# Sliding-window attention with sinks and an RWKV channel mix on one Trainium2 core: the attention band packed into 64-key pieces, the value product in 64 x 64 tiles

## The chip, the core and the metric

The kernel runs on one core of a Trainium2 chip. The engines of that core work side by side and wait for each other by semaphores: PE (TensorE, matrix products, with its weight loads shown apart as PEld), DVE (VectorE), ACT (ScalarE), POOL (GpSimd) and SP (SyncE, which here only issues transfers). PE holds weights of up to 128 x 128 and streams the other operand past them; it can also be used as four quadrants of 64 x 64, each with weights and a stream of its own. The array's results go to PSUM, from which DVE and ACT read. Transfers between HBM and the on-chip SBUF run on 16 DMA engines.

The metric is the device time of the kernel in microseconds (us), the median of several runs, for the slowest core (here the only one).

## What is computed

```python
def _attn_ref(q, k, v, n_sink, window):          # B, H, S, D = 4, 8, 768, 64
    scale = 1.0 / np.sqrt(D)
    scores = scale * np.matmul(q, k.transpose(0, 1, 3, 2))
    pos = np.arange(S)
    is_sink = pos[None, :] < int(n_sink)         # n_sink = 4
    rel = pos[:, None] - pos[None, :]
    in_window = (rel >= 0) & (rel < int(window)) # window = 128
    scores = np.where(is_sink | in_window, scores, -1000000000.0)
...
    a = np.exp(scores)                           # softmax over the keys
...
    return np.matmul(a, v)

def _moe_ref(x, mu_k, mu_r, w_k, w_v, w_r):      # x: 4 x 768 x 512, heads side by side
    x_prev = ...                                 # x of the token before, zero at the start
    xk = mu_k * x + (1.0 - mu_k) * x_prev
    xr = mu_r * x + (1.0 - mu_r) * x_prev
    k = np.maximum(xk @ w_k, 0.0)                # 512 x 1024
    v = k * k @ w_v                              # 1024 x 512
    r = 1.0 / (1.0 + np.exp(-(xr @ w_r)))        # 512 x 512
    return r * v
```

The kernel's mask also keeps the four sink keys for queries that lie before them in the first rows, as the reference does. Inputs and output are float32, all matrix products run in bf16.

## The kernel before

The 4 sequences of 768 tokens are cut into 12 units of 256 queries: unit u is part T = u % 3 of sequence b = u // 3. The 8 heads go in 4 pairs (c or k in the code); a pair's two heads lie on the two halves of the 128 rows. A unit passes through four stages.

*Prepare.* Loads bring q, k and v of the unit as float32 (tiles qs, ks, vs, issued by SP at L462, L472, L479, L486). Casts to bf16 (qb, kb: L689, L693, L698; vb with an added column of ones: L770) run on ACT, POOL or DVE. Then q and k are transposed so that the head dimension lies on the rows (qt, kt): on PE (L733, L738), with an evacuation from PSUM, or, for k from unit 5 and q from unit 7 on, by a DMA transpose issued on SP (L715).

*Attend.* The scores are computed with keys on the rows and queries along the columns (tile sc in PSUM, two heads side by side, 512 columns each): L845, on 64 x 64 tiles (in unit 0 with whole 128-key weights). For one pair and each of the two heads, the 512 columns hold four blocks of 128 keys by 128 queries: the two diagonal blocks, the block one below, and the block that looks back into the unit before. Two pairs are done together. The exponential is taken by ACT (L917: 128 x 1024 elements, or 128 x 768 in a sequence's first unit, where nothing lies behind), and DVE multiplies the whole tile e by a mask of zeros and ones (L931). The value product L950 takes e as weights, 128 keys by 128 queries, and streams v with its column of ones, so that column 64 of the result is the softmax's denominator: 16 matmuls of 65 columns for two heads and 2 x 128 queries (12 in a first unit) add up in a PSUM bank. The four sink keys come in separately for T = 1 and 2 (scores L814 or L821, values L888 with whole-array weights or L903 in tiles), before the value product and into the same bank. DVE takes the reciprocal (L964) and multiplies (L967) into x.

*Mix.* x is transposed (on PE at L991, or by DMA at L1011) into xt; DVE forms td = x - x_prev (L1027) and the mixes xk and xr (L1040).

*Channel mix.* Key product L1117 (weights of 128 x 128 from w_k, 256 tokens streamed, 32 matmuls a unit), relu (L1127 on ACT or L1131 on DVE), square (L1139, DVE), gate product L1148, tanh (L1154, ACT; the sigmoid is got from it), value product L1166 (16 matmuls of 512 columns a unit), the final product with the gate (L1175, DVE; L1087 and L1097 are the last unit's own copies), and the store (L1182, L1102).

What sets the order: every operation gets a number as the program is built, and a table ORDER lists for each engine the numbers in the order in which it issues them; SP's list orders the loads, DMA transposes and stores. A table CHOICE says which engine takes an operation that has alternatives (a cast, a copy from PSUM, a relu, "PE/full" or "PE/tiles" for the sinks). The planner walks the lists with a table of costs, only to decide which buffer of a pool each tile gets: there are 2 score tiles sc, 5 tiles e, 4 PSUM banks for everything else, 3 staging tiles for each of q, k and v. An operation waits for its inputs and for its buffer. The weights come as float32 too: w_k in two halves of 1 MB (cast at L650 and L656, 128 x 1024 elements a piece), then w_r (1 MB) and w_v in two halves of 1 MB, all issued on SP at L505 through three staging tiles w.

```python
            P.op("ACT", act(width), expo, r, take=[("e", ek)], hold=[sck], reads=[sck],
                 writes=[ek])
...
            if u not in BIAS:
                P.op("DVE", dve(width, 0.52), masked, r, hold=[ek], port=True, writes=[ek],
                     reads=["mask" if T else "mask0"])
...
                            nc.tensor.matmul(out=o[:, g, a, :], lhsT=e[:, a, e0:e0 + 128],
                                             rhs=rhs, start=(T == 0 and i == 0),
                                             stop=(i == len(blocks) - 1), skip_group_check=True)
```

BIAS is empty in the kernel before, so that every unit has its mask. `take` claims a buffer, `hold` keeps one until the operation is done, `reads` and `writes` name what is waited for.

## Time and profile before

| | us | share of the span |
|---|---|---|
| timed runs: median of 3 (lowest to highest) | 166.36 (165.06 to 167.31) | |
| the profiled execution, span from first to last instruction | 163.8 | |
| PE busy | 154.4 | 94% |
| DVE busy | 148.4 | 91% |
| ACT busy | 121.4 | 74% |
| POOL busy | 32.7 | 20% |

The profiled execution shows only its span. What lies around the span (start and end of the kernel) is in the timed runs alone; against their median it is 2.5 us.

The page's second part cuts the span in 40 slices of 4.1 us; a digit is the busy share in tenths.

```profile
PE   7989779899999999999999999999999999999991
DVE  2589999999999999999999999998898989999931
ACT  3779899999999998999996689882499694152020
POOL 6643543222731022111103001032000100101001
```

PE has some free time in the first seven slices and next to none after; DVE is full from the fourth slice to the last but two; ACT has room in the second half, POOL nearly everywhere. A share of 91 or 94% alone doesn't say which engine sets the end: for that, the stretches and the chain of waits are needed.

How to read the rows that follow. In a row of the group view stand line, engine, operation, output<-inputs, shape and count, then after the bar the busy time of all in us and the mean duration of one in ns, and after the second bar the engine's idle time just ahead of them, with what ended it. A row of the time line has start, duration, engine, line and operation, both times in us. A row of the chain of waits has start, duration, engine, what is written and the line. A row of transfers has the output<-input, the queue that issued it, the count, the size of each and the median time from issue to landing. "SPq" is SP's queue as an issuer of transfers.

### The profile page before, as it was taken

Reading aid. Unit: us, or ns where it says so; the run is one execution under the profiler, and the core shown is the slowest. Engines: PE = TensorE matmul, PEld = TensorE weight load, DVE = VectorE, ACT = ScalarE, POOL = GpSimd, SP = SyncE. Lnnn points to the kernel's source line nnn. Section 1 sums busy time; section 2 is a strip of 40 time slices with the busy share of each in tenths; the row PEclk is TensorE's granted clock in tenths of the full one; section 3 lists DMA queues with packets and bytes.
Section 4 is the critical chain, followed back from the end, with each engine's and each line's share of the span. In section 5 each row is a group of like instructions: output and inputs, shape, how many; then the busy total and the mean of one; then the engine's idle time right before and its main releaser. Section 6 shows DMA issues by size and latency. Waiting matters only on the chain.

```text
span 163.8 us, 4680 instructions
## 1 busy us (share of the span) xinstructions
PE 154.4 (94%) x1845; PEld 100.8 (62%) x1845; DVE 148.4 (91%) x383; ACT 121.4 (74%) x198; POOL 32.7 (20%) x61
## 2 busy tenths in 40 slices
PE   7989779899999999999999999999999999999991
...
DVE  2589999999999999999999999998898989999931
ACT  3779899999999998999996689882499694152020
POOL 6643543222731022111103001032000100101001
...
GB/s 138 250 334 275 400 346 205 362 397 338 200 289 238 265 233 225 196 179 189 276 233 174 254 196 218 242 188 119 239 162 201 268 79 98 57 203 64 0 144 112
DMA packets 78821, 35.16 MB, mean 215 GB/s; under 512 B 68744, under 2 KB 71056, under 8 KB 78800
## 3 DMA queue, kind: packets, MB, share of 16 engines
...
q0 software_dynamic: 400, 1.31, 2.3%
q8 instruction: 14, 0.23, 0.6%
q14 instruction: 7, 0.06, 0.1%
q10 hardware_dynamic: 16, 0.00, 0.0%
HBM read 24.12 MB, written 6.29 MB: 186 GB/s over the span
## 4 chain that ended last, share of the span: by engine, by line
PE 69%; DVE 11%; DMA 10%; SPq 5%; issue 2%; ACT 1%; POOL 0%; DVEq 0%; POOLq 0%
PE bank L1117 22%; PE bank L1166 19%; PE bank L1148 9%; PE bank L950 6%; DMA ks<-in_k_dram 5%; PE sc L845 4%; DMA kt<-kb 4%; DVE e L931 3%; SPq L462 3%; PE bank L1232 3%; DVE xk L1040 2%; DVE x L967 2%; PE bank L903 1%; SPq L479 1%; PE bank L991 1%
## 5 line engine op out<-in xcount | busy, mean ns | idle before, releaser
L1117 PE MATMUL bank<-xk,wk_sb 128*128 128x256 bf16 x384 | 47.3, 273 | 0.7 <-ACT rl L1127 0.5
L917 ACT ACTIVATE e<-sc 128x1024 bf16<-128x1024 f32 (+1 forms) x48 | 44.4, 966 | 3.4 <-PE sc L845 3.3
L1166 PE MATMUL bank<-wv_h,kk 128*128 128x512 bf16 x184 | 44.9, 379 | 0.0
L1117 PEld LDWEIGHTS <-wk_sb 128*128 128x128 bf16 x384 | 36.2, 98 | 7.0 <-issue 0.9
L931 DVE TENSOR_TENSOR e<-e,mask 128x1024 bf16<-128x1024 bf16 (+1 forms) x48 | 31.7, 676 | 0.0
L1127 ACT ACTIVATE rl<-bank 128x512 bf16<-128x512 f32 x43 | 25.1, 606 | 8.1 <-PE bank L1117 7.9
L1154 ACT ACTIVATE th<-bank 128x512 f32<-128x512 f32 x24 | 14.3, 608 | 18.2 <-PE bank L1148 11.4
L1166 PEld LDWEIGHTS <-kk 128*128 128x128 bf16 x184 | 17.0, 98 | 16.4
L1148 PE MATMUL bank<-wr_sb,xr 128*128 128x512 bf16 x96 | 23.8, 379 | 0.0
L1040 DVE SCALAR_TENSOR_TENSOR xk<-td,mu_all,xt 128x256 bf16<-128x256 bf16 x48 | 23.2, 511 | 0.0
L1040 DVE SCALAR_TENSOR_TENSOR xr<-td,mu_all,xt 128x256 bf16<-128x256 bf16 x48 | 22.4, 477 | 0.0
L967 DVE TENSOR_TENSOR x<-bank,rec 128x256 bf16<-128x256 f32 x48 | 19.5, 418 | 0.5
L1139 DVE TENSOR_TENSOR kk<-rl 128x512 bf16<-128x512 bf16 x48 | 19.3, 416 | 0.3 <-ACT rl L1127 0.2
L1175 DVE SCALAR_TENSOR_TENSOR ob<-th,bank 128x512 f32<-128x512 f32 x23 | 15.6, 682 | 2.4 <-PE bank L1166 1.1
L950 PE MATMUL bank<-vb,e 128*128 128x65 bf16 x352 | 16.5, 194 | 0.3
L950 PEld LDWEIGHTS <-e 128*128 128x128 bf16 x352 | 13.8, 97 | 3.5 <-DVE e L931 0.7
L1148 PEld LDWEIGHTS <-xr 128*128 128x128 bf16 x96 | 9.0, 98 | 9.6
L845 PE MATMUL sc<-qt,kt 64*64 64x128 bf16 (+3 forms) x496 | 12.6, 226 | 0.4 <-DMA kt<-kb 0.3
L1182 POOL DMA_DIRECT2D out_dram<-ob x5 | 2.8, 570 | 47.0 <-DVE ob L1175 47.0
L845 PEld LDWEIGHTS <-kt 64*64 64x64 bf16 (+1 forms) x496 | 9.0, 106 | 4.1 <-issue 1.4
L1027 DVE TENSOR_TENSOR td<-xt 128x512 bf16<-128x512 bf16 x24 | 10.1, 433 | 0.1
L770 ACT CAST vb<-vs 128x512 bf16<-128x512 f32 x14 | 8.8, 636 | 0.2 <-DMA vs<-in_v_dram 0.2
...
## 6 DMA issues: line engine op xcount, KB each, us to landing
vs<-in_v_dram SPq DMA_DIRECT2D x24, 256.0 KB, 5.5
out_dram<-ob SPq DMA_DIRECT2D x18, 256.0 KB, 3.4
ks<-in_k_dram SPq DMA_DIRECT2D x16, 256.0 KB, 4.6
qs<-in_q_dram SPq DMA_DIRECT2D x12, 256.0 KB, 4.7
...
w<-in_moe_w_k_dram SPq DMA_DIRECT2D x2, 1024.0 KB, 8.8
w<-in_moe_w_v_dram SPq DMA_DIRECT2D x2, 1024.0 KB, 11.3
```

What stands on the lines that cost most here:

```text
L845: nc.tensor.matmul(out=sc[keys, a, o0 + f0 - q0:o0 + f1 - q0], lhsT=lhs[rows, keys], rhs=qs[rows, f0:f1], start=u not in BIAS, stop=True, ...
L917: nc.scalar.activation(out=buf[ek][:, :, lo:], in_=buf[sck][:, :, lo:], func=AF.Exp, scale=scale)
L931: nc.vector.tensor_tensor(out=at, in0=at, in1=m, op=ALU.mult)
L950: nc.tensor.matmul(out=o[:, g, a, :], lhsT=e[:, a, e0:e0 + 128], rhs=rhs, start=(T == 0 and i == 0), stop=(i == len(blocks) - 1), skip_gro ...
L967: P.op("DVE", dve(256), lambda ok=ok, rk=rk, c=c: nc.vector.tensor_tensor(out=buf["x", u][:, :, 128 * c:128 * c + 128].rearrange("p g (a d ...
L1040: nc.vector.scalar_tensor_tensor(out=buf[key][:, c, :], in0=buf[tk][:, i, :], scalar=mu[w][:, c:c + 1], in1=xt[:, c, t0 - 1:t0 + 255], op0 ...
L1117: nc.tensor.matmul(out=ps[:, i, :], lhsT=wk_sb[:, c, 128 * f:128 * f + 128], rhs=xk[:, c, :], start=(c == 0), stop=(c == NC - 1), skip_gro ...
L1127: nc.scalar.activation(out=buf[rk], in_=buf[psk].rearrange("p (i t) -> p i t", i=2), func=AF.Relu)
L1139: P.op("DVE", dve(512, 0.52), lambda f2=f2, rk=rk: nc.vector.tensor_tensor(out=buf["kk", u][:, 2 * f2:2 * f2 + 2, :], in0=buf[rk], in1=buf ...
L1148: nc.tensor.matmul(out=buf[psk], lhsT=buf["xr", u][:, c, 128 * g:128 * g + 128], rhs=wr_sb[:, c, :], start=(c == 0), stop=(c == NC - 1))
L1166: nc.tensor.matmul(out=buf[psk], rhs=wv_h[:, f, :], lhsT=buf["kk", u][:, f, 128 * g:128 * g + 128], start=(f == 0), stop=(f == NF - 1))
L1175: P.op("DVE", dve(512), lambda psk=psk, tk=tk, bk=bk: nc.vector.scalar_tensor_tensor(out=buf[bk], in0=buf[tk], scalar=1.0, in1=buf[psk], o ...
```

## The change

**Packing.** The band of 128 keys back is cut into pieces of 64 keys by 64 queries. For each head, and for each half h of the 128 rows (even 64-key blocks on rows 0 to 63, odd ones on rows 64 to 127), six such pieces lie side by side in 384 columns, at places given by a table `slot`. Pieces that lie outside the band have no place any more. In each half the pieces at places 0, 3 and 2, 5 are the triangles (the edge of the window, seen from either side); places 1 and 4 need no mask. So sc is used for 2 x 384 columns instead of 2 x 512, e has that size, the exponential always takes 128 x 768 elements (L1005), and the mask multiplies only 2 x 2 x 2 x 64 = 512 elements a row (L1015).

**Triangles by matmul.** In units 0, 1 and 2 (BIAS) there is no mask. There, 4 more matmuls a pair (48 in all, on 64 x 64 tiles, 256 columns each, L898) add -30000 to the triangles in PSUM, ahead of the exponential. The tables for this are made on POOL at the start, with the new masks; the identity now comes before them.

**Values in tiles.** The value product (L923) takes e as weights of 64 keys by 64 queries and streams 65 columns of v: 24 matmuls a pair (20 in a first unit) instead of 8 (6), on the four quadrants. Two pairs are done in two halves: in the first, key rows 0 to 63 work on the first pair and rows 64 to 127 on the second; in the second half, the other way about, into the same PSUM bank rows. Between the halves stands `tick`, a memset of one element on POOL (L1026), made to wait for the first half's last matmul; the second half's first matmul is made to wait for it.

**Sinks** all go in tiles ("PE/tiles"). WHOLE is gone: unit 0 too is done in tiles.

**Order.** ORDER, CHOICE and the places where PE's instruction fetches are expected (FETCH) are new throughout. Five stores that POOL issued go to SP ("SP" in CHOICE). PE has 5376 instructions (weight loads among them) where it had 3679.

```diff
+BIAS = (0, 1, 2)
...
-BIAS = ()
...
-WHOLE = (0,)
...
-    pool("e", 5, [128, 2, 512], BF16)
+    pool("e", 5, [128, 2, 384], BF16)
...
+    def behind(one, other):
+        tc.add_manual_dep(one.ins, other.ins.name, mybir.DependencyInfo(
+            mybir.DependencyClass.Sync, mybir.DependencyReason.DATA))
...
+    scratch = tile1([1, 1], FP32, "scratch")
...
+        slot = [{(0, 0): 0, (0, 1): 1, (0, 2): 2, (2, 2): 3, (2, 3): 4},
+                {(1, 1): 0, (1, 2): 1, (1, 3): 2, (3, 3): 3}]
+        if T > 0:
+            slot[0][-2, 0] = 5
+            slot[1][-1, 0], slot[1][-1, 1] = 4, 5
+        else:
+            slot[0][0, 3] = 5
...
+            spans = [[(0, 0, 3), (2, 2, 4)], [(1, 1, 4), (3, 3, 4)]]
...
+                        nc.tensor.matmul(
+                            out=sc[64 * h:64 * h + 64, a, c0:c0 + 64 * (i1 - i0)],
+                            lhsT=keys[rows, k, kb // 2 % 2, 64 * h:64 * h + 64],
+                            rhs=qs[rows, 64 * i0:64 * i1], start=u not in BIAS or n == 0,
+                            stop=u not in BIAS, skip_group_check=u in BIAS)
+            if u not in BIAS:
+                return
+            for a in range(2):
+                rows = slice(64 * a, 64 * a + 64)
+                for h in range(2):
+                    nc.tensor.matmul(
+                        out=sc[64 * h:64 * h + 64, a, 0:384].rearrange(
+                            "p (t s w) -> p t s w", t=2, s=3)[:, :, 0:3:2, :],
+                        lhsT=ident[rows, rows],
+                        rhs=(bias[rows].unsqueeze(1).to_broadcast([64, 2, 2, 64]) if T else
+                             bias0[rows, h]), start=False, stop=True, skip_group_check=True)
...
+        def values(cs, second):
+            todo = [[], [], [], []]
+            for h in range(2):
+                c = cs[(h + second) % 2]
+                for (kb, i), n in sorted(slot[h].items(), key=lambda x: (x[0][1], x[0][0])):
+                    for a in range(2):
+                        todo[2 * h + i % 2].append((kb, i, n, a, c))
...
+                        new = nc.tensor.matmul(
+                            out=buf["o", u, c][64 * m:64 * m + 64, o0:o0 + D + 1],
+                            lhsT=buf["e", u, c][rows, a, 64 * at:64 * at + 64],
+                            rhs=buf["vb", u if kb >= 0 else u - 1][rows, kb // 2 % 2, 2 * c + a, :],
+                            start=T == 0 and not second and (c, m) not in begun,
+                            stop=bool(second), skip_group_check=True)
+                        if second and not begun:
+                            behind(new, halves[u, cs[0]])
...
-            P.op("ACT", act(width), expo, r, take=[("e", ek)], hold=[sck], reads=[sck],
+            P.op("ACT", act(768), expo, r, take=[("e", ek)], hold=[sck], reads=[sck],
...
+                at = buf[ek].rearrange("p a (t s w) -> p (a t) s w", t=2, s=3)[:, :, 0:3:2, :]
+                m = (mask.unsqueeze(1).to_broadcast([128, 4, 2, 64]) if T else
+                     mask0.rearrange("p a t s w -> p (a t) s w"))
...
-                P.op("DVE", dve(width, 0.52), masked, r, hold=[ek], port=True, writes=[ek],
+                P.op("DVE", dve(512, 0.52), masked, r, hold=[ek], port=True, writes=[ek],
...
+                        def tick(at=(u, cs[0])):
+                            new = nc.gpsimd.memset(scratch, 0.0)
+                            behind(new, halves[at])
+                            halves[at] = new
```

The first place that the new order moves is SP's queue of loads at the start, before the channel mix. The first listing shows the rows of the kernel before around the loads of w_k (w_76 and w_77 are the staging tiles; ks, qs, vs are those of k, q and v; the names in brackets are the semaphores that the issue waits for).

```order
L479 DMA ks_69<-in_k_dram 128x2x512 [waits DMAHW5_49]
L505 DMA w_76<-in_moe_w_k_dram 128x4x512 [waits DMAHW6_49]
L505 DMA w_77<-in_moe_w_k_dram 128x4x512 [waits DMAHW7_49]
L479 DMA qs_70<-in_q_dram 128x2x512 [waits DMAHW0_49,DVE_49,Activation_49]
L462 DMA vs_75<-in_v_dram 128x8x64 [waits DMAHW1_49]
L462 DMA vs_75<-in_v_dram 128x8x64 [waits DMAHW2_49]
L479 DMA ks_67<-in_k_dram 128x2x512 [waits DMAHW3_49,Pool_49]
L505 DMA w_78<-in_moe_w_r_dram 128x4x512 [waits DMAHW4_49]
```

The second listing shows the same queue of the changed kernel, from the third unit's loads to w_r.

```order
L507 DMA ks_67<-in_k_dram 128x2x512 [waits DMAHW6_49,DVE_49]
L490 DMA vs_75<-in_v_dram 128x8x64 [waits DMAHW7_49]
L507 DMA qs_71<-in_q_dram 128x2x512 [waits DMAHW0_49,Activation_49,Pool_49]
L490 DMA vs_75<-in_v_dram 128x8x64 [waits DMAHW1_49]
L507 DMA qs_70<-in_q_dram 128x2x512 [waits DMAHW2_49,Pool_49]
L533 DMA w_76<-in_moe_w_k_dram 128x4x512 [waits DMAHW3_49]
L507 DMA qs_72<-in_q_dram 128x2x512 [waits DMAHW4_49,Activation_49,Pool_49]
L507 DMA ks_68<-in_k_dram 128x2x512 [waits DMAHW5_49]
L533 DMA w_77<-in_moe_w_k_dram 128x4x512 [waits DMAHW6_49]
```

w_k's first half has moved behind the loads of ks_67, both of vs_75, qs_71 and qs_70; its second half also behind qs_72 and ks_68. Ahead of the first half stand 6.0 MB where 4.0 stood, and the two halves no longer stand together.

The second place is POOL in the middle of the program, around the copies of the third sequence's sink keys (ksink from kt). Before, POOL has only casts (kb, qb, vb) and copies there.

```order
L693 CAST kb_79<-ks_67 128x4x128 [waits DMAHW6_49,DVE_49,PE_49]
L770 CAST vb_136<-vs_75 128x8x64 [waits DMAHW1_49]
L787 COPY ksink_151<-kt_87 64x4x4 [waits DMAHW4_49]
L787 COPY ksink_151<-kt_87 64x4x4 [waits Pool_49]
L693 CAST kb_80<-ks_68 128x4x128 [waits PE_49,DMAHW5_49,Activation_49,Pool_49]
L693 CAST kb_81<-ks_69 128x4x128 [waits DMAHW3_49,DMAHW0_49]
L693 CAST qb_84<-qs_72 128x4x128 [waits DMAHW5_49,PE_49,Activation_49]
```

In the changed kernel the ticks stand between them in the same queue.

```order
L729 CAST qb_82<-qs_70 128x4x128 [waits DMAHW2_49,DMAHW5_49,DVE_49,Activation_49]
L1026 MEMSET scratch 1x1 [waits PE_49,Pool_49]
L823 COPY ksink_154<-kt_87 64x4x4 [waits DMAHW4_49]
L823 COPY ksink_154<-kt_87 64x4x4 [waits Pool_49]
L729 CAST qb_84<-qs_72 128x4x128 [waits DMAHW0_49,Pool_49]
L1026 MEMSET scratch 1x1 [waits PE_49]
L1026 MEMSET scratch 1x1 [waits PE_49,Pool_49] x2
L729 CAST qb_83<-qs_71 128x4x128 [waits DMAHW1_49,Activation_49]
L1026 MEMSET scratch 1x1 [waits PE_49,Pool_49] x2
```

Each memset waits for PE, stands behind whatever cast POOL issues before it, and is waited for by the first weight load of a second half on PE; six of the 24 come before PE's first matmul of the channel mix, 18 after.

251 lines of the change are left out of this document (134 added, 117 removed), and 141 rows, old and new, of the table ORDER.

## The prediction

> **What bounds the kernel now.** I read the page's first lines, then cut the span at two events: the first matmul of the channel mix (L1117, its key product) and the first value product (L1166).
>
> ```profile
> span 163.8 us, 4680 instructions
> L1117 PE MATMUL bank<-xk,wk_sb x384: 269/273/283, 24.3 to 151.4; 128*128 128x256 bf16 x192
> L1166 PE MATMUL bank<-wv_h,kk x184: 377/379/390, 41.1 to 158.6; 128*128 128x512 bf16 x184
> 0.00:24.30 24.30, 19.77 (x242) 11.32 (x243) 19.07 (x55) 18.68 (x29) 12.47 (x32) 1.00 0.97 291
> 24.30:41.10 16.80, 15.94 (x215) 11.77 (x211) 16.73 (x44) 16.27 (x27) 4.51 (x5) 1.00 1.03 323
> 41.10:160.30 119.20, 118.72 (x1396) 77.75 (x1394) 112.03 (x285) 86.47 (x144) 15.38 (x26) 1.00 0.87 186
> 21.52 1.31 DVE e L931 x2
> ```
>
> The two rows with "x384:" and "x184:" give when those lines first ran. The three rows of stretches give start and end, length, the busy time of PE, its weight loads, DVE, ACT and POOL, the granted clock (1.00 is full), the DMA share and GB/s; the last row is one of the chain of waits. They say: up to 24.3 us PE waits (its busy time there holds warm-up matmuls) and the chain of waits runs through DVE, the masks of L931 among it; from 24.3 to 41.1 PE, DVE and ACT are all full; from 41.1 to 160.3 PE is busy 118.72 of 119.20 us. So after the first channel-mix matmul the end is PE's own work, and a microsecond saved on DVE or ACT there is worth nothing by itself. The sum is: when PE can begin the channel mix, plus what PE has to do from there.
>
> **Prices on PE.** Consecutive starts in the time line, and merged rows of the chain, give what one group occupies.
>
> ```profile
> 57.92 0.31 PE L903 MATMUL bank<-vsink,es 64*64 64x130 bf16 x8
> 58.06 0.51 PE L845 MATMUL sc<-qt,kt 64*64 64x192 bf16 x24
> 58.50 0.66 PE L950 MATMUL bank<-vb,e 128*128 128x65 bf16 x16
> 59.00 0.39 PE L733 MATMUL bank<-ident,qb 128*128 128x128 bf16 x4
> 59.22 0.38 PE L1166 MATMUL bank<-wv_h,kk 128*128 128x512 bf16 x1
> 49.16 1.31 PE bank L1117 x12
> 56.27 1.73 PE bank L1148 x8
> 70.63 0.23 PE bank L888 x4
> 58.17 0.40 PE L845 MATMUL sc<-qt,kt 64*64 64x128 bf16 x16
> ```
>
> Eight tiled sink matmuls take 0.14, 24 tiled scores 0.44, 16 value matmuls of 128 x 128 0.50 (0.031 each), four transposes 0.22, a channel-mix matmul 0.109 (L1117) or 0.216, four full sinks 0.23. Switching between 64 x 64 tiles and the whole array costs about 0.09: the last scores end at 58.57 (58.17 + 0.40), and the first whole-array matmul starts 0.07 before that, whereas within one mode a matmul starts 0.16 before its predecessor ends (379 ns of duration against 216 of spacing). So the scores themselves are 0.35. Each of the four quadrants streams 768 columns in them: 0.456 ns a column.
>
> **The values.** A half now is 24 matmuls of 65 columns on four quadrants (20 in a sequence's first unit); the busiest quadrant has 8 (6), so 520 (390) columns: 0.237 (0.178), against 0.50 (0.38) for the 16 (12) before, which two halves replace. Values alone are a gain of 0.03 per two pairs. What is added with them is a round trip in the middle: the second half starts only after a POOL memset that waits for the first half.
>
> ```profile
> 58.72 0.76 POOL L693 CAST kb<-ks 128x512 bf16<-128x512 f32 x1 [5.32 <-PE sc L845]
> 0.34 0.10 POOL L1271 MEMSET const-float32-1.0<- 128x1 f32 x1
> 7.47 0.61 POOL L698 CAST kb<-ks 128x512 bf16<-128x512 f32 x1 [1.52 <-DMA ks<-in_k_dram]
> 8.13 0.40 PE L738 MATMUL bank<-ident,kb 128*128 128x128 bf16 x4 [0.38 <-POOL kb L698]
> L950 PE MATMUL bank<-vb,e 128*128 128x65 bf16 x352 | 16.5, 194 | 0.3
> ```
>
> POOL starts 0.15 after the scores' end (58.57), a memset takes 0.10, PE starts 0.05 after a POOL instruction's end (7.47 + 0.61), and a 65-column matmul ends 0.19 after its start: 0.49 for the trip. Of the 18 trips after the first channel-mix matmul, 16 have the next two pairs' scores between the halves (0.35 and 0.02 of spacing), one the sink scores and one two products. So 17 expose about 0.12, **2.1** in all (between 0, if PE pulls its weights early, and 0.3 each). Behind a second half wait the rest of PE's queue, and DVE's reciprocals and x (L964, L967).
>
> **PE's work after the first channel-mix matmul**, counted in PE's order: the three products of the channel mix are the same. Values go from 296 to 36 halves (24 of the larger kind): 9.2 becomes 7.8, so -1.4. Score groups go from 19 to 17, -0.7. Transposes (L733, L991) go from 92 to 60, -1.8. Three full sink groups go and one tiled comes, -0.5. Switches go from 44 to 49, +0.5. Together **-3.9**: this work now stands ahead of that matmul, or is gone. The triangles by matmul (48, in units 0 to 2) are all ahead of it. So are 15 of 20 added switches.
>
> **When that matmul can start.** Its weights now stand behind 6.0 MB of loads, not 4.0.
>
> ```profile
> 13.68 1.16 SPq L505 DMA_DIRECT2D w<-in_moe_w_k_dram  x2
> w<-in_moe_w_k_dram SPq DMA_DIRECT2D x1, 1024.0 KB, 7.8
> 15.62 4.56 SPq L462 DMA_DIRECT2D vs<-in_v_dram  x2
> vs<-in_v_dram SPq DMA_DIRECT2D x2, 256.0 KB, 10.9
> 25.49 0.72 SPq L505 DMA_DIRECT2D w<-in_moe_w_r_dram  x1
> w<-in_moe_w_r_dram SPq DMA_DIRECT2D x1, 1024.0 KB, 7.0
> 22.45 1.11 ACT L650 ACTIVATE wk_sb<-w 128x1024 bf16<-128x1024 f32 x1
> ```
>
> Each pair of rows is an issue and its time to landing. The first half of wk landed at 21.5 as the fifth megabyte; the seventh was complete with v of unit 2, the second transfer of its row, at about 27.2; w_r, with which 8.5 MB were complete, at 32.5. The queue was full throughout (DMA share 0.97 and 1.03), so I take landing by bytes: wk's first half, now megabyte seven, at 27.2, its cast 1.1 later, the matmul at 28.4 and not 24.3: **+4.1** (+2 if the queue fills sooner, +6 if PE still has attention to do). Its second half completes megabyte nine, half a megabyte after the last mark: 1.6 later at 323 GB/s, so 34.1, castable by 35.2; PE wants it after 32 key matmuls, two transpose groups, a score group, more transposes and sink scores, 5.3 later (33.7): **+1.5**. Against that, PE's work between the two events before came to 15.0 by the prices above in 16.8 us; those 1.8 of waits were for weights and for masks and go, **-1.8**. Of PE's later waits I take off **0.5** for faster ACT and DVE:
>
> ```profile
> L1117 PE MATMUL bank<-xk,wk_sb 128*128 128x256 bf16 x384 | 47.3, 273 | 0.7 <-ACT rl L1127 0.5 <-DVE xk L1040 0.2
> L917 ACT ACTIVATE e<-sc 128x1024 bf16<-128x1024 f32 x32 | 31.8, 1037 | 2.2 <-PE sc L845 2.1
> L917 ACT ACTIVATE e<-sc 128x768 bf16<-128x768 f32 x16 | 12.6, 825 | 1.2 <-PE sc L845 1.2
> L931 DVE TENSOR_TENSOR e<-e,mask 128x1024 bf16<-128x1024 bf16 x32 | 22.9, 727 | 0.0
> L931 DVE TENSOR_TENSOR e<-e,mask 128x768 bf16<-128x768 bf16 x16 | 8.9, 573 | 0.0
> L1139 DVE TENSOR_TENSOR kk<-rl 128x512 bf16<-128x512 bf16 x48 | 19.3, 416 | 0.3 <-ACT rl L1127 0.2
> ```
>
> The exponentials fall to 48 of 825 ns (-6.8). The masks fall from 31.8 to 36 of 512 elements, 0.42 each by the equally long kk row (-16.7); casts, copies and relus that now run on DVE give back about 8. Both gains lie beside PE's work after 28.4, where that work covers them; ahead of it they let PE finish three units' attention instead of two and a half, which the -3.9 holds already.
>
> Sum: 163.8 + 4.1 + 1.5 - 1.8 - 0.5 - 3.9 + 2.1 = 165.3, and 0.3 for the one short-covered trip (sink scores, 0.22): 165.6. The three timed runs have a median of 166.36 and run from 165.06 to 167.31, 2.5 above the span at the median. Adding 1.8 to the median gives 168.2: no change that a measurement can tell, since about 2% (163.0 to 169.7) is what it can.
>
> **The rivals.**
>
> *Faster: the front wins.* The early loads here are mostly 2-KB pieces, so the queue may fill sooner: the matmul at 26.4 (-2.0), no wait for the second half (-1.5), the trips hidden (-2.4): 162.3. For it speaks that the first stretch's DMA share was 0.97 with 291 GB/s against 323 in the second; against it, that all three must come together.
>
> *Slower: the memset is stuck in POOL's line.* Nine of the 18 memsets stand directly behind a cast or copy that waits for a load or another engine.
>
> ```profile
> POOL vb L770 <- DMA vs<-in_v_dram: 19.9, 5, 12.6
> L693 POOL CAST kb<-ks 128x512 bf16<-128x512 f32 x6 | 4.0, 664 | 19.7 <-DMA ks<-in_k_dram 10.4 <-PE sc L845 7.4 <-ACT xt L1000 1.9
> ```
>
> The first row gives POOL's waits for v (sum, count, longest): up to 12.6 us at a time, and that cost nothing; now PE waits with it. It decides once a load lands after the first half of the values: nine casts of 0.6 on average are +5.0: 173.2.
>
> *Slower: the tiles' weights.* Only the sinks reload all four quadrants in every wave, at 0.07 a wave; were a value wave to take that, halves cost 0.56 and 0.42, +10: 178. The scores, with 24 loads in 0.35, speak against it.
>
> The Trainium skill (TensorEngine Tiling (Array Packing), Gotcha 2: Feature Incompatibilities) says that column tiling excludes the fast weight load, and its page TensorE: Matmul & The Clock Gate (LDWEIGHTS) puts a load at one column per cycle of 1.2 GHz, 53 ns for 64 columns. By that estimate a wave would last 53 ns and not 30, and the kernel 174.7; the trace's loads of 14 ns apiece in the scores do not bear it out, but there only some quadrants reload at once.
>
> *Slower: the last keys.* The last unit's first scores have 33.0 us of PE work behind them by these prices, 29.7 before.
>
> ```profile
> 125.30 1.23 SPq L715 DMA_TRANSPOSE kt<-kb  x1
> kt<-kb SPq DMA_TRANSPOSE x7, 3.9
> 130.36 0.46 PE sc L845 x16
> ```
>
> Their transpose was issued at 125.3, to land by about 129; a PE that ends at 162.1 wants them at 128.9. Five stores more on that queue could make it 3 later: 171.
>
> *The relief does nothing.* If DVE and ACT relief is worth more than I took, 166: still no change.
>
> **Chances.** Forecast 0.45; the front 0.18; POOL's line 0.19; tile weights 0.07; last keys 0.06; more relief 0.05. So faster 0.18, within 2% 0.45 + 0.05 = 0.50, slower 0.32. The range runs from the front's 162.0 to POOL's 173.5; outside lie the tile weights and parts of the two rivals at its ends, under 0.2. Over the forecast's own terms it is 165 to 170.
>
> **What would show it.** The first channel-mix matmul at 28.4 rather than 24.3; between halves some 0.12 of PE idle, released by POOL; values near 0.24 a half; PE busy to the end with DVE near 85% of the span. I am wrong if PE has gaps of half a microsecond behind POOL, if wk lands near 21, or if value waves come slower than 30 ns.

## The result, and the profile after

The changed kernel takes 177.38 us (median of 4 runs, 175.44 to 178.61), the kernel before 166.62 us on the same chip: slower by a ratio of 1.062 (95% interval 1.053 to 1.071). The forecast was 168.2, with a range up to 173.5. (Ratios here leave out executions that were disturbed, so one can lie a little below the ratio of its medians.)

First the answers that correspond to those shown of before: the page's head of the changed kernel, the row of the channel mix's key product (L1187, which was L1117), and the stretches. The stretches are cut at the first transposes, the first transpose of x, the first key product, the first value product (L1236, which was L1166) and PE's end; the columns are those of the prediction.

```profile
span 175.8 us, 6387 instructions
...
PE 160.1 (91%) x2673; PEld 107.1 (61%) x2695; DVE 141.3 (80%) x382; ACT 109.5 (62%) x185; POOL 32.8 (19%) x98
```

```profile
L1187 PE MATMUL bank<-xk,wk_sb x384: 272/273/283, 37.8 to 165.1; 128*128 128x256 bf16 x192
```

```profile
0.00:7.55 7.55, 4.63 (x7) 2.00 (x7) 3.31 (x17) 2.10 (x3) 5.89 (x26) 1.00 0.70 203
7.55:20.89 13.34, 11.84 (x220) 8.25 (x219) 6.33 (x15) 8.71 (x14) 6.64 (x22) 1.00 1.14 308
20.89:37.80 16.91, 12.70 (x406) 9.87 (x405) 12.87 (x36) 12.38 (x21) 4.49 (x12) 0.90 0.82 293
37.80:54.85 17.05, 16.59 (x222) 12.90 (x222) 16.29 (x41) 15.30 (x26) 5.41 (x7) 1.00 0.95 259
54.85:172.30 117.45, 114.38 (x1828) 74.12 (x1846) 102.08 (x275) 70.96 (x122) 10.34 (x32) 1.00 0.87 170
```

The same cut of the kernel before, where its first stretch of 24.3 us is split in three:

```profile
0.00:4.70 4.70, 3.57 (x4) 1.27 (x5) 1.70 (x8) 1.50 (x3) 3.38 (x14) 1.00 0.53 154
4.70:12.63 7.93, 6.86 (x63) 3.81 (x62) 5.71 (x21) 6.35 (x10) 3.67 (x12) 1.00 1.04 298
12.63:24.30 11.67, 9.34 (x179) 6.25 (x177) 11.67 (x28) 10.83 (x18) 5.42 (x6) 1.00 1.11 342
```

The first key product came at 37.8 us and not at 24.3: 13.5 later, of which 2.85 stand ahead of the first transposes, 5.4 ahead of the first transpose of x and 5.2 behind it. From there to PE's end it is 134.5 us, 136.0 before, so that part gained 1.5. The span grew by 12.0, which is 13.5 less 1.5. The whole loss lies ahead of the channel mix, and there PE was idle: busy 12.70 of 16.91 in the third stretch, while DVE, full before (11.67 of 11.67), also waited.

What PE waited for: first its time line around the two largest gaps (start, length, operation; in brackets the idle time in front and its cause), then SP's with the loads of weights, the time from issue to landing of w_k's first half, and the casts of w_k (lengths in ns, first and last start).

```profile
24.72 0.36 PE L888 MATMUL sc<-qt,kt 64*64 64x192 bf16 x12
26.59 0.30 PE L898 MATMUL sc<-bias,ident 64*64 64x256 bf16 x4 [1.51 <-issue]
...
30.80 0.28 PE L898 MATMUL sc<-bias,ident 64*64 64x256 bf16 x4
32.79 0.31 PE L991 MATMUL bank<-vsink,es 64*64 64x130 bf16 x8 [1.70 <-ACT qb L725]
```

```profile
20.20 0.60 SPq L533 DMA_DIRECT2D w<-in_moe_w_k_dram  x1
...
23.48 0.78 SPq L533 DMA_DIRECT2D w<-in_moe_w_r_dram  x1
37.23 0.37 SPq L533 DMA_DIRECT2D w<-in_moe_w_v_dram  x1
```

```profile
w<-in_moe_w_k_dram SPq DMA_DIRECT2D x1, 1024.0 KB, 7.6
```

```profile
L686 ACT ACTIVATE wk_sb<-w x2: 1060/1060/1060, 36.1 to 42.4; 128x1024 bf16<-128x1024 f32 x2
```

The first half of w_k was issued at 20.20 and landed 7.6 later, at 27.8, yet its cast began only at 36.1: the weights lay there for 8 us, and the channel mix waited for something else. In the first gap nothing that the profile shows was waited for ("issue", between instructions of one score group). The second gap is put down to a cast that has nothing to do with sinks. Both fall on a pattern that appears when PE's instructions (weight loads and matmuls) are counted in order and the packets of the instruction queue (q8, 16 KB each) are set beside them. The table is worked out from the traces: the number of the instruction, when the one ahead of it started, the gap up to it, and the first fetch after it; the fetch that ends a gap stands a row higher.

```
kernel    instr.  reached   gap    next fetch
before       449    22.90   0.00   25.70-26.86
before       705    33.25   0.11   36.08-37.14
after        449    20.26   0.41   24.26-25.31
after        705    24.89   1.70   30.45-31.57
after        961    30.81   1.97   33.94-34.88
```

The gaps fall on instructions 449, 705 and 961, 256 apart, which is 16 KB a block. PE resumed 1.3 and 1.2 us after the end of a fetch (25.31 to 26.59, and 31.57 to 32.78). That this is no accident shows in all the traces of this case together: they hold 28 gaps of over 1 us at these numbers and at 1217, in 13 runs, and every one ends 1.2 to 1.6 us after the end of a fetch, whatever the other engines have just finished. Blocks came about 6 us apart (24.26, 30.45), and each fetch began 3.6 to 3.9 us after PE had entered a block (20.67, 26.59), while loads kept the DMA engines full. The kernel before reaches its first key product as instruction 488, the changed one as 1259: small tiles mean many instructions, and half a unit more of attention stands ahead.

One thing more stands in the third stretch: the granted clock is 0.90 there, which was 1.00 throughout before. In steps of 2 us:

```profile
32.00:34.00 2.00, 1.21 (x58) 0.89 (x58) 0.27 (x1) 1.44 (x3) 0.09 (x1) 1.00 0.94 342
34.00:36.00 2.00, 1.74 (x40) 1.38 (x38) 1.90 (x7) 1.41 (x3) 0.00 (x0) 0.57 0.15 59
36.00:38.00 2.00, 2.00 (x74) 1.92 (x66) 2.00 (x6) 1.21 (x3) 1.36 (x4) 0.57 0.04 8
38.00:40.00 2.00, 2.00 (x23) 1.81 (x22) 1.94 (x7) 2.00 (x4) 1.95 (x3) 1.00 0.59 208
```

From 34 to 38 us PE runs at 0.57 of its clock (0.5 in the middle), right behind its gaps. The same rows show the loads run dry (8 GB/s): SP stood at the load of w_v from 24.3 to 37.2 us, since its staging tile held the w_k that was not yet cast.

### The profile page after: what moved, and what is told of

Its sections match the earlier page's. It is cut to its first block, busy times and chain, and to the rows that moved or that the text cites. A ratio compares the mean times of both kernels' runs of the same rounds, so it can differ in the third digit from the quotient of the medians.

```text
span 175.8 us, 6387 instructions
## 1 busy us (share of the span) xinstructions
PE 160.1 (91%) x2673; PEld 107.1 (61%) x2695; DVE 141.3 (80%) x382; ACT 109.5 (62%) x185; POOL 32.8 (19%) x98
## 4 chain that ended last, share of the span: by engine, by line
PE 70%; DMA 9%; DVE 7%; issue 4%; POOL 3%; ACT 2%; SPq 2%; DVEq 0%; POOLq 0%; ACTq 0%
PE bank L1187 19%; PE bank L1236 18%; PE bank L1218 10%; PE bank L923 8%; PE sc L888 4%; DMA kt<-kb 3%; PE bank L769 3%; DMA ks<-in_k_dram 3%; DMA qt<-qb 3%; DVE xr L1110 2%; PE bank L1061 2%; PE bank L991 2%; POOL hmask L604 1%; SPq L1081 1%; PE sc L898 1%
## 5 line engine op out<-in xcount | busy, mean ns | idle before, releaser
L1187 PE MATMUL bank<-xk,wk_sb 128*128 128x256 bf16 x384 | 48.7, 273 | 0.0
L1236 PE MATMUL bank<-wv_h,kk 128*128 128x512 bf16 x172 | 43.9, 379 | 1.7 <-DVE kk L1209 0.7
L1005 ACT ACTIVATE e<-sc 128x768 bf16<-128x768 f32 x48 | 37.7, 814 | 8.0 <-PE sc L898 4.4
L1187 PEld LDWEIGHTS <-wk_sb 128*128 128x128 bf16 x384 | 36.6, 98 | 9.6
L1197 ACT ACTIVATE rl<-bank 128x512 bf16<-128x512 f32 x37 | 21.5, 599 | 24.5 <-PE bank L1187 21.3
L1236 PEld LDWEIGHTS <-kk 128*128 128x128 bf16 x184 | 17.2, 98 | 18.2 <-DVE kk L1209 0.7
L1110 DVE SCALAR_TENSOR_TENSOR xr<-td,mu_all,xt 128x256 bf16<-128x256 bf16 x48 | 23.8, 506 | 0.0
L923 PE MATMUL bank<-vb,e 64*64 64x65 bf16 x1088 | 20.7, 197 | 1.2 <-DVE kt L787 0.7
L923 PEld LDWEIGHTS <-e 64*64 64x64 bf16 x1088 | 16.3, 109 | 5.7 <-issue 2.3
L1026 POOL MEMSET scratch<- 1x1 f32 x24 | 2.5, 105 | 89.7 <-PE bank L923 86.0
L946 DVE RECIPROCAL rec<-bank 128x4 f32<-128x4 f32 x48 | 7.1, 171 | 11.0 <-PE bank L923 10.7
L888 PE MATMUL sc<-qt,kt 64*64 64x64 bf16 (+2 forms) x544 | 15.4, 226 | 0.5 <-DMA kt<-kb 0.4
L1015 DVE TENSOR_TENSOR e<-e,mask 128x512 bf16<-128x512 bf16 x36 | 14.5, 418 | 0.0
L888 PEld LDWEIGHTS <-kt 64*64 64x64 bf16 x544 | 12.1, 110 | 2.2 <-DVE kb L734 0.8
```

What stands on the lines that cost most here:

```text
L888: nc.tensor.matmul(out=sc[64 * h:64 * h + 64, a, c0:c0 + 64 * (i1 - i0)], lhsT=keys[rows, k, kb // 2 % 2, 64 * h:64 * h + 64], rhs=qs[rows ...
L923: new = nc.tensor.matmul(out=buf["o", u, c][64 * m:64 * m + 64, o0:o0 + D + 1], lhsT=buf["e", u, c][rows, a, 64 * at:64 * at + 64], rhs=bu ...
L1005: nc.scalar.activation(out=buf[ek], in_=buf[sck][:, :, 0:384], func=AF.Exp, scale=scale)
L1015: nc.vector.tensor_tensor(out=at, in0=at, in1=m, op=ALU.mult)
L1110: nc.vector.scalar_tensor_tensor(out=buf[key][:, c, :], in0=buf[tk][:, i, :], scalar=mu[w][:, c:c + 1], in1=xt[:, c, t0 - 1:t0 + 255], op0 ...
L1187: nc.tensor.matmul(out=ps[:, i, :], lhsT=wk_sb[:, c, 128 * f:128 * f + 128], rhs=xk[:, c, :], start=(c == 0), stop=(c == NC - 1), skip_gro ...
```

## The experiments

Each kernel is the changed kernel with the edit shown, and lines of code may be shifted by it (L1187 is L1194 or L1200 below). "First key product" is the start of its first matmul in the one profiled execution. Times are medians, with the ratio to the kernel before in the same session and its 95% interval. How far a single start can be trusted shows in the changed kernel itself: a second profile of it, further down, has 37.04 where the first has 37.80.

**GpSimd's constants.** Before the change POOL built ident first; after it, the triangles and masks stand ahead of it (rows of the changed kernel, then of before):

```profile
1.28 0.92 POOL L604 TENSOR_SCALAR_AFFINE_SELECT mask<-ones 64x64 bf16<-64x64 bf16 x4 [0.77 <-DVE ones L588]
2.25 0.92 POOL L604 TENSOR_SCALAR_AFFINE_SELECT bias<-warm 64x64 bf16<-64x64 bf16 x4
3.25 2.11 POOL L604 TENSOR_SCALAR_AFFINE_SELECT hmask<-hmask 128x260 bf16<-128x260 bf16 x4
...
6.86 0.28 POOL L604 TENSOR_SCALAR_AFFINE_SELECT ident<-ones 128x128 bf16<-128x128 bf16 x1
```

```profile
2.31 0.28 POOL L573 TENSOR_SCALAR_AFFINE_SELECT ident<-ones 128x128 bf16<-128x128 bf16 x1
```

Identity first, in the order of POOL's operations (72 is ident, 75, 76 and 78 are masks):

```diff
-        75, 73, 78, 76, 72, 79, 74, 132, 101, 77, ...
+        72, 75, 73, 78, 76, 79, 74, 132, 101, 77, ...
```

> Changed kernel with one move on POOL: the identity is made first, ahead of the masks, the triangles and hmask. Theory A (POOL's constants hold up the front): the identity is ready near 2.1 us instead of 7.5, the first transposes start near 5.1 (when k's first cast ends) instead of 7.55; but the triangles of unit 0 (bias0) are still ready only near 9.3, and the first scores, at 10.27 before, wait for them, so the first channel-mix matmul comes only 0 to 1 us earlier than 37.8, and the time falls by 0 to 1 from 177.4. Theory B (the forecast: w_k's landing and cast set that matmul) and theory C (the attention of three units that PE's order puts ahead of it sets it): no change, first channel-mix matmul 37.5 to 38.

Identity first and the band's masks behind the first units' casts:

```diff
-        75, 73, 78, 76, 72, 79, 74, 132, 101, 77, ..., 141,
+        72, 73, 74, 78, 79, 132, 101, 77, ..., 141, 75, 76,
```

> Changed kernel with POOL's order changed at the start: identity, triangles of units 0 to 2, hmask, then the casts of q; the masks, which no unit before the fourth reads, go behind the first cast of v of unit 1. Theory A: bias0 is ready near 4.6, first transposes near 5.1, first scores near 7.2 instead of 10.27, POOL's casts of q near 7 and 8 instead of 9.4 and 10.0; the first channel-mix matmul at 33.5 to 35.5 instead of 37.8 and the time 2.5 to 4.5 lower, near 174. Theory B: the first half of w_k lands near 27.8 as before and its cast follows; no change. Theory C: the chain of attention is set by its own round trips and by the loads; less than 1 us lower.

177.41 us (1.068, 1.063 to 1.073) and 179.07 (1.075, 1.068 to 1.081). The first transposes came at 4.71, where they were before the change, but the first key product at 37.69 and 37.73, not at the 33.5 to 35.5 that theory A gave for the second: 2.8 us won at the start were gone 30 us later. The gaps had moved with the work: 1.09, 1.87 and 1.78 at instructions 705, 961 and 1217 in the first of the two. Something paces PE that a sooner start does not speed up.

**The weights.** The two loads of w_k right behind the second unit's v on SP's queue:

```diff
-        1, 0, 7, 3, 2, 6, 4, 5, 16, 15, 10, 11, 19, 17, 20, 18, 24, 8, 29, 23, 9,
+        1, 0, 7, 3, 2, 6, 4, 5, 16, 15, 10, 11, 8, 9, 19, 17, 20, 18, 24, 29, 23,
```

> Changed kernel with the two loads of w_k moved in SP's queue to where they stood before the change, right behind the loads of unit 1 and k of unit 2; k, q and v of units 2, 3 and 4 land later by up to 2 MB (6 to 7 us). Theory B: w_k lands near 21 and 25 instead of 27.8, and the first channel-mix matmul moves up by 4 us or more: time near 173. Theories A and C: w_k isn't waited for; v of unit 2 and q and k of unit 3 land 3 to 6 us later and hold up the attention that PE's order has ahead of the channel mix: first channel-mix matmul between 37.8 and 44, time 177.4 to 183.

179.04 us (1.068, 1.059 to 1.078), first key product at 38.14. The first half of w_k landed at 21.48 instead of 27.77, and the channel mix began no earlier. The landing of w_k, from which the prediction set that start, does not hold it.

**The trips.** Each tick made twice as long by a second memset:

```diff
+                            new = nc.gpsimd.memset(scratch, 0.0)
                             new = nc.gpsimd.memset(scratch, 0.0)
```

> Changed kernel with two memsets in a row on POOL instead of one between the two halves of the values: each round trip is about 0.1 us longer. If the trips are exposed as the forecast had it (0.12 each in 17 of 18 places behind the first channel-mix matmul, and in the 6 ahead of it), 23 trips of 0.1 more give +2.3, near 179.7. If the scores between the halves hide the trip with room to spare (theories A and C, in which the front is the whole loss): less than +0.8. If PE waits in POOL's line (forecast's rival): more than +2.3, since what stands behind a memset in POOL's queue is late too.

180.04 us (1.073, 1.065 to 1.081). The medians are 2.7 apart, where 2.3 followed from the forecast's exposures, but the ratios (1.073 and 1.062) only 1.8, with intervals that overlap, so the time alone doesn't settle it. The traces do. The step from the last matmul ahead to the first of a second half is 0.275 us behind scores, where the changed kernel has 0.129, and the 18 such steps behind the first key product add up to 5.5 us against 2.9. The longer trip comes out in PE's order almost everywhere: the trips are on the path. Ahead of the first key product they aren't what holds it, which stayed at 37.74.

**The supply of instructions.** More of them, ahead of the first key product, in two ways. First 128 matmuls of one column behind the scores of the second and third unit:

```diff
+            if u in (1, 2):
+                for i in range(16):
+                    nc.tensor.matmul(out=sc[0:64, 0, 384:385], lhsT=ident[0:64, 0:64],
+                                     rhs=ident[0:64, 0:1], start=True, stop=True, ...
```

> Changed kernel with 128 tiny matmuls more (64 x 64 weights, one column, into columns of the score tiles that nobody reads) in units 1 and 2, all ahead of the first channel-mix matmul: 256 PE instructions, one block of 16 KB. Theory F (PE's instructions come in blocks of 256; under the full queue of loads a block is asked for when PE enters the block before it and lands some 5 to 6 us later, so that PE cannot go through the front faster than about 6 us a block): first channel-mix matmul 4.5 to 6.5 us later than 37.8, near 43, and the time near 182 to 183. Theory C (round trips of the attention set the front, PE has time to spare there: 11 us of warm-up matmuls): only PE's own time counts, 128 at 0.02 or less, so 0 to 2.6 us.

184.72 us (1.100, 1.089 to 1.110), first key product at 42.97, now instruction 1515. This is inconclusive. The matmuls took 0.032 us each at the full clock and 0.053 at half of it, 5.3 us of PE's own time in all, which is about as much as the supply of 256 instructions. And the clock was halved from 20.0 to 37.0 us, with PE busy throughout:

```profile
20.00:37.00 17.00, 16.71 (x310) 12.67 (x309) 9.41 (x27) 7.37 (x13) 3.50 (x8) 0.50 0.92 322
```

So the second way adds instructions without columns: the triangles of those units by 16 matmuls of 64 columns and not 4 of 256.

```diff
+            if T:
+                for t in range(4):
+                    for a in range(2):
+                        rows = slice(64 * a, 64 * a + 64)
+                        for h in range(2):
+                            o0 = (0, 128, 192, 320)[t]
+                            nc.tensor.matmul(
+                                out=sc[64 * h:64 * h + 64, a, o0:o0 + 64],
+                                lhsT=ident[rows, rows], rhs=bias[rows, t % 2, :],
+                                start=False, stop=True, skip_group_check=True)
+                return
```

> Changed kernel in which the triangles of units 1 and 2 are added by 16 matmuls of 64 columns a pair instead of 4 of 256: the same columns on the same quadrants, 96 matmuls and 192 PE instructions more ahead of the first channel-mix matmul. PE's own time: 24 matmuls with their loads take 0.35 in the scores, 15 ns each, so 96 more are at most 1.4, spread over eight pairs. Theory F: 192 instructions are three quarters of a block, 4.4 at 5.9 us a block: first channel-mix matmul near 42 (40.5 to 43) with gaps at every block from 449 on, time near 181.5. Theory C: 0 to 1.4 later: 37.8 to 39.2, time 177.4 to 179.

183.71 us (1.100, 1.093 to 1.107), first key product at 41.35 as instruction 1451: 192 instructions more, 3.6 us later, with gaps of 1.46, 3.17 and 1.64 us at instructions 449, 961 and 1217. That fits the supply, and theory C gave 1.4 at most. But in this profile PE also ran at half clock in four stretches of 3.4 us each, where the changed kernel has one, so neither the 3.6 us at the start nor the 6 us of time are the supply's alone.

Then fewer transfers ahead of each fetch, in two ways. Without the loads of w_k's second half and of w_r (this kernel leaves out all but a sliver of these two loads, so it computes with weights that are not theirs):

```diff
+            if (name, i) in (("wk", 1), ("wr", 0)):
+                return lambda: queue.dma_start(out=buf[key][:, 0:1, 0:16], in_=src[:, 0:1, 0:16])
...
+        kept = key
+        if name != "wv":
+            key = ("w32", "wk", 0)
...
```

> Changed kernel that leaves out the loads of w_k's second half and of w_r (a few bytes each are loaded instead, and the casts read w_k's first half in their place): 2 MB fewer in the queue between 23 and 36 us. Nothing ahead of the first channel-mix matmul reads them, and PE's instructions are the same. Theory F: the fetches that follow 26 us find an emptier queue and land 1 to 3 us earlier; the stall of 1.97 at PE instruction 961 goes, that of 1.70 at 705 may stay; first channel-mix matmul 35 to 36.5, time 1.5 to 3 lower. Theories A and C: that matmul stays at 37.3 to 38; the time falls only by what the second half of w_k was waited for later, 0 to 1.

The first key product came at 35.87, within what was expected, but this run doesn't show why: of the 1.9 us, 1.6 were there when PE reached instruction 449 (19.07 against 20.67), ahead of the loads that are left out, and the gap at 961 only shrank from 1.97 to 1.04. The time did not fall (179.62, 1.075, 1.067 to 1.084). And with all loads, but from the 11th on each waiting until the third before it has landed:

```diff
+    def fly(new):
+        if 10 <= len(flown) < 28:
+            behind(new, flown[-3])
+        flown.append(new)
...
-            return lambda: queue.dma_start(out=buf[key], in_=src)
+            return lambda: fly(queue.dma_start(out=buf[key], in_=src))
```

> Changed kernel in which, from the eleventh load on, each load on SP waits until the third load before it has landed (three under way instead of up to eight); order, bytes and all other instructions are the same. Theory F: a block of PE instructions asked for under a shorter queue of loads is there after some 4 us instead of 5.9 to 6.2; the gaps at PE instructions 449, 705 and 961 (0.4, 1.7, 2.0 us) shrink to under 0.5 each, the first channel-mix matmul comes at 33.5 to 36 and the time is 2 to 4 lower, near 174.5, if the loads don't land later by more than that. Theory C (round trips of the attention): the loads land no earlier, so the first channel-mix matmul stays at 37.5 or later, time 177 or more. If the fetch doesn't depend on the depth of the queue, the gaps stay.

175.59 us (1.058, 1.049 to 1.068), first key product at 34.85, 3.0 sooner than in the changed kernel's first profile and 2.2 sooner than in its second. The same instructions in the same order now met gaps of 0.00, 0.02 and 0.40 us at 449, 705 and 961, and one of 1.78 at 1217. The loads ahead of it landed at most 0.6 us sooner, and w_k's first half later (30.60 instead of 27.77), so it isn't that the operands came earlier: a fetch that finds fewer loads in front comes in time. Of the 3.0 us, 1.7 were won behind instruction 449, where the gaps were.

Now GpSimd's order could tell. Short queue, identity first, the band's masks behind operation 264:

```diff
-        75, 73, 78, 76, 72, 79, 74, 132, ..., 264, 194,
+        72, 73, 74, 78, 79, 132, ..., 264, 75, 76, 194,
```

> As e8_short_queue, and POOL's start in another order: identity, triangles, hmask, then the casts; the two masks behind the cast of q of unit 3. Theory F with A: with the fetches out of the way the earlier start on POOL (first scores near 7 instead of 10.3) is no longer eaten up: first channel-mix matmul 31 to 34.5, time 2 to 3 below that of e8_short_queue. Theory F with POOL's start of no importance: as e8_short_queue. Theory C: POOL's order alone gave nothing in e2_pool_order and gives nothing here: 37 or later.

174.28 us (1.049, 1.039 to 1.059), first key product at 32.92. What moved nothing by itself moves it by 1.9 us once the supply lets it.

**What the triangles by matmul are worth.** The masks of the first three units on DVE again, as in the other units:

```diff
-BIAS = (0, 1, 2)
+BIAS = ()
...
-        70, 71, 92, 94, 98, 134, 81, 103, 131, ...
+        70, 71, 92, 94, 2001, 98, 134, 81, 103, 2000, 131, ...
```

(2000 to 2011 are the twelve masks in DVE's order.)

> Changed kernel without the triangles by matmul: units 0 to 2 have masks on DVE as the others do; 48 matmuls (96 PE instructions) and the tables bias and bias0 on POOL (0.92 and 1.4 us) go, 12 masks of 0.42 us come to DVE ahead of the first channel-mix matmul. Theory F: 96 instructions at 6 us a block of 256 are 2.2 us: first channel-mix matmul near 35.5, time near 175. Theory C: 12 masks more in the round trips (two a group, 0.8 us in each of six groups, half of it covered): first channel-mix matmul 38 to 41, time 178 to 180. Theory A (POOL's tables): 2.3 us earlier on POOL, as much at most for the first channel-mix matmul.

179.08 us (1.063, 1.054 to 1.071), first key product at 39.80, 2.0 later than with the triangles, although 94 instructions fewer stood ahead of it. This was a miss for the supply as the only pace, which gave 35.5. What held it instead is not separated: PE still stood 1.57 and 2.39 us at instructions 449 and 705, and in this profile the clock was halved from 30.4 to 40.6 us, for three times as long as in the changed kernel. The four runs spread from 176.87 to 182.27, and by the ratio (1.063 against 1.062) the time is the same. So that the triangles by matmul are a gain isn't shown.

**A new plan.** A search over the orders and the engines of casts and copies, with the measured prices of POOL and the blocks of 256, alone and with the short queue:

```diff
-    89: "ACT", 90: "ACT", 91: "DVE", 92: "DVE", 94: "DVE", 95: "ACT", ...
+    89: "DVE", 90: "DVE", 91: "ACT", 92: "DVE", 94: "ACT", 95: "POOL", ...
```

> Changed kernel with the same instructions in another order on every engine and other choices of engine for casts and copies: found by a search over orders, with POOL's constants at their measured durations (8.4 us in all instead of 5.6) and PE's instructions in blocks of 256 that take 3.2 to 6.1 us to come. Identity and triangles come first on POOL, the loads of w_k move up behind v of unit 2, and the channel mix begins nearer the end of unit 1's attention. If the loss lies in the order at the front and in the supply of instructions there (theories A and F), and not in the tiles, ticks and small pieces themselves: first channel-mix matmul 28.5 to 32.5, time 168 to 173. If the pieces and tiles cost what was lost in any order: 175 or more.

> As e11_replanned, and from the eleventh load on each load waits until the third before it has landed. Theory F: what gaps are left at PE's blocks (instructions 449 to 1217) shrink by 0.5 to 1.5 each, first channel-mix matmul 0 to 2 us earlier than in e11_replanned; the weights behind it land later, so the time changes by -2 to +1.

180.88 us (before: 165.85) and 179.84 (1.082, 1.078 to 1.087), with the first key products at 35.80 and 32.69. The first missed on both numbers (with the clock halved from 23.8 to 37.4 us); the second came 3.1 us sooner at the start, for 0 to 2 expected, and 1.0 in time. It met no gap at any block, but needed 142.0 us from the first key product to PE's end. An early start is not enough where the plan behind it is worse.

**Where the front's gain goes.** The changed kernel and the kernel with short queue and GpSimd's order in one session:

> The changed kernel as it is, on the same chip and in the same rounds as the two others: ratio to the kernel before 1.06 to 1.07, first channel-mix matmul 37.3 to 38.1 under every theory.

> e10_short_queue_pool once more, beside the changed kernel on one chip. Theories F and A: 2 to 4 us faster than the changed kernel in these rounds. If its 174.3 was the chip or the day: within 1 us of it.

177.9 us (1.072, 1.067 to 1.077) and 176.45 (1.060, 1.054 to 1.066), with first key products at 37.04 and 33.09. The first is 0.3 sooner than expected under every theory, and the gain of 1.45 in time lies between the two expectations. In the profiled executions the lead of 4.0 us was 2.5 at the 128th key product (70.86 and 73.38) and gone by 135 us, from where the second kernel was 0.8 behind; its chain of waits runs there through loads of v and transposes of k. Was it the stand of SP at w_v's load? w_v (operations 13 and 14) behind the loads of three more tiles:

```diff
-        12, 13, 21, 22, 14, 27, 28, 25, 34, 26, 32, ...
+        12, 21, 22, 27, 28, 13, 25, 26, 14, 34, 32, ...
```

> The changed kernel with the loads of the two halves of w_v moved behind the loads of v3, k5 and v4 on SP's queue, so that SP no longer stands from 24.3 to 37.2 us at w_v's load, which waits for the casts of w_k. Theory G (that stand lets the load queue run dry at 35 to 40 us, and 1.9 MB less than before have come by 60 us, which the end pays for): the hole in the row of DMA at 35 to 40 us goes, at least 16.3 MB have come by 60 us (15.1 in the changed kernel, 17.0 before), the first channel-mix matmul stays at 36.5 to 38, and the time falls by 1 to 3 us, to 174.5 to 176.5. The rival (PE's own front alone sets the time): the hole goes, but the time stays within 1 us of the changed kernel's 177.4.

The same with GpSimd's order and the short queue, here up to the 20th load:

> All three at once: w_v's loads later (as in the run beside it), the identity ahead of the masks on GpSimd, and each of the 11th to the 20th load waiting for the third before it. If the supply of instructions, the masks ahead of the identity and the hole in the loads each cost their part: the first channel-mix matmul at 32.5 to 34.5 us and the time 170 to 173 us. If the hole costs nothing: the same first matmul and 175 to 176.5 us, as with the other two alone. If the short queue takes from the transfers what the moved loads give: under 16 MB by 60 us and 176 us or more.

179.26 us (1.079, 1.076 to 1.083) and 174.9 (1.049, 1.043 to 1.055), with first key products at 37.7 and 33.8. The theory fell: the hole was not closed but moved (from 34 to 38 us to 52 to 60). These are stretches of the kernel with w_v later alone:

```profile
0.00:20.00 20.00, 14.75 (x229) 9.39 (x229) 9.59 (x32) 10.99 (x18) 12.48 (x48) 0.91 0.97 263
20.00:35.00 15.00, 12.04 (x378) 9.21 (x378) 11.95 (x35) 11.90 (x21) 3.50 (x10) 0.89 1.08 365
35.00:60.00 25.00, 22.95 (x333) 16.59 (x330) 19.74 (x52) 19.24 (x32) 6.25 (x12) 0.93 0.63 174
```

By length times GB/s 15.1 MB had come by 60 us, no more than in the changed kernel (15.3), whose queue ran dry sooner and then caught up. I read this as loads that can't run further ahead than the staging tiles that the work frees; no run tests it. What did change is the clock: 0.91, 0.89 and 0.93 in three stretches, against 0.98 and 0.95 in the second and third of the changed kernel. This pointed to the next theory.

**The order ahead of the channel mix.** In the kernel with short queue and GpSimd's order, the first key products moved ahead of part of the third unit's attention on PE, and DVE's and ACT's casts of w_k's first half (82 and 83) moved up in their orders; on SP a load of q (20) and one of v (18) changed places:

```diff
-        174, 262, 176, 268, 202, 265, 195, 250, 240, 243, 245, 348, 271, 354, 251,
-        254, 320, 256, 278, 209, 210, 296, 430, ...
+        174, 262, 176, 268, 202, 265, 195, 250, 240, 243, 245, 271, 251, 254, 209,
+        210, 320, 256, 213, 214, 278, 348, 354, 296, 430, ...
...
-        1, 0, 7, 3, 2, 6, 4, 5, 16, 15, 10, 11, 19, 17, 20, 18, 24, 8, 29, 23, 9,
+        1, 0, 7, 3, 2, 6, 4, 5, 16, 15, 10, 11, 19, 17, 18, 20, 24, 8, 29, 23, 9,
```

> The short queue and GpSimd's order as before (first channel-mix matmul at 32.8 to 33.0 us, 174.3 and 176.5 us in two runs), and beside them the first key matmuls of the channel mix moved ahead of the last four query transposes, sink scores and value halves of the third unit on TensorE, and the DVE's half of w_k's cast ahead of the last query cast. If it is the attention ahead of it in TensorE's order that now holds the channel mix (w_k's half landed at 29.2 us): the first matmul at 30 to 31.5 us, and, if the start is what counts, 172 to 174.5 us. The rival (from that start on the loads and the chain through the last keys set the end, as 136.4 us from the first matmul to TensorE's end against 134.5 hint): the first matmul as early, 137.5 us or more from there to the end, and 174.5 to 176.5 us.

A miss on both numbers: 179.15 us (1.072, 1.067 to 1.078), first key product at 33.66. The first half of w_k landed at 31.36 and not at 29.2; DVE stood at its cast until then, and what the channel mix needs from DVE came behind it, with the clock halved from 29.6 to 36.4 us:

```profile
31.39 0.69 DVE L699 CAST wk_sb<-w 128x1024 bf16<-128x1024 f32 x1 [5.65 <-DMA w<-in_moe_w_k_dram]
...
33.66 1.86 PE L1194 MATMUL bank<-xk,wk_sb 128*128 128x256 bf16 x8 [1.93 <-DVE x L956]
```

So here the landing of w_k does take part in the start: with the short queue it comes late enough to matter once the order no longer does.

**The clock.** In the kernel with short queue and GpSimd's order PE is busy half of 24 to 30 us, and from 30 to 34 us its clock is 0.57. To that kernel 11 matmuls on zeros were added in PE's waits between 23 and 30 us:

```diff
+AWAKE = {202: 1, 240: 6, 354: 4}
...
+            for _ in range(AWAKE.get(i, 0)):
+                name, j = next(x[1:3] for x in own if x[1] in ("bank", "sc"))
+                to = self.pools[name][j]
+                order.append(("fill", to if name == "bank" else to[:, 0, :], 1))
```

> The kernel with the short queue and GpSimd's order, and beside them 11 matmuls on zeros (512 columns, 0.22 us each) where TensorE waits between 23 and 30 us. In all profiles of that kernel and its kin the granted clock is 0.5 for some 3.4 us from about 30 us on, right behind that stretch of waits (here at 30 to 34 us), which costs 1.65 us of TensorE's work; the kernel before never shows it. Theory H (the idle places of the longer front let the clock fall, and the halved clock is a part of the loss): the clock stays at 1.00 from 20 to 60 us, the first channel-mix matmul comes at 31.5 to 32.5 us, and the time is 172.5 to 174.5 us, against 174.3, 176.5 and 174.9 in three runs of the same front without these matmuls. The rival (TensorE waits there for loads and DVE anyway): the clock stays up and the time is 174.5 to 176.5 us. If the half clock comes for another reason: it is at 30 to 34 us as before.

The kernel without them, then with them:

```profile
24.00:30.00 6.00, 3.08 (x106) 2.40 (x106) 4.05 (x11) 4.83 (x9) 3.65 (x15) 1.00 0.99 370
30.00:34.00 4.00, 3.83 (x90) 3.19 (x90) 3.87 (x12) 2.38 (x4) 2.22 (x5) 0.57 0.86 290
```

```profile
24.00:30.00 6.00, 4.58 (x112) 2.90 (x110) 4.37 (x12) 4.30 (x8) 3.11 (x13) 1.00 1.04 379
30.00:34.00 4.00, 4.00 (x107) 3.40 (x106) 4.00 (x11) 3.20 (x5) 1.87 (x5) 1.00 0.87 281
```

```profile
L1200 PE MATMUL bank<-xk,wk_sb x384: 269/273/283, 32.1 to 160.7; 128*128 128x256 bf16 x192
```

The clock stayed at 1.00, the first key product came at 32.1 and PE ended at 167.9, against 169.3. In time it was 174.49 us (1.042, 1.035 to 1.049), on the border between theory and rival. The ratio is the lowest of all changed kernels, but its interval overlaps those of the same front without the matmuls (1.039 to 1.059, 1.043 to 1.055; 1.054 to 1.066 lies apart), and the median of the first of those was 174.28, no higher. That PE's waits bring the fall is shown, as only they were filled. That it is worth anything in time here is not. (The half clock lasts longer than the 3.4 us of the expectation in some kernels of this kind: 6.8 us in the two runs above with w_v later and with the first key products early.) No version came near the time before.

## Why the prediction was wrong

**The step that failed** is "When that matmul can start". It priced the wait for w_k's first half and read the start off its landing. The landing was right (27.2 forecast, 27.8 measured); the start was 37.8 and not 28.4. The clause "+6 if PE still has attention to do" had named the cause but bounded it by 2 us, without counting what three units' attention needs ahead of that matmul: 1259 instructions instead of 488. The work that moved there was priced at nothing, on the reason that faster DVE and ACT "let PE finish three units' attention instead of two and a half". The term of +4.1 was +13.5. What showed in its place: the weights lay landed for 8 us, their casts came only at 36.1 behind the attention's copies and products, and w_k landing at 21.48 left the start at 38.14. The runs take the 13.5 apart so:

| part | shown by | us at the first key product |
|---|---|---|
| short queue: mostly the supply of instructions | 37.80 to 34.85 | 3.0 |
| masks and triangles ahead of the identity on POOL | 34.85 to 32.92, with the short queue | 1.9 |
| halved clock behind PE's waits | 32.92 to 32.13 with matmuls in them | 0.8 |
| the rest: three units' attention, its loads, casts and banks | not taken apart | 7.8 |

So 5.7 us are taken apart and 7.8 stay open. The 4.1 that the forecast put down to the landing is none of these parts, as the landing doesn't hold the start. The parts come from one order of removals, and in another they would differ (POOL's was 0 while supply held). Each is a difference of single profiles, and two profiles of one kernel differ by 0.8 (37.80 and 37.04) or 0.2 (32.92 and 33.09), so the smallest part is not clear of that. The rest was tried by order alone, and that failed.

**From the start to the end** the forecast was near: 28.4 to 162.1 is 133.7, measured 134.5. PE's busy time there (the last two stretches) is 131.0 where it was 134.7, 3.7 less for the -3.9 foreseen. *Values*: 24 matmuls of a half took 0.252 from first to last start by the trace, for 0.237. By the 8 on the busiest quadrant that is 31.5 ns a wave, just over the 30 that the forecast had set as a sign of being wrong; the tiles' weights, with 0.56 for a half, can be ruled out. *Trips*: behind scores, the step to a second half is 0.129 where one within the mode is 0.02, so 0.11 for 0.12, as here:

```profile
68.11 0.51 PE L888 MATMUL sc<-qt,kt 64*64 64x192 bf16 x22
68.40 0.09 POOL L1026 MEMSET scratch<- 1x1 f32 x1 [4.90 <-PE bank L923]
...
68.55 0.45 PE L923 MATMUL bank<-vb,e 64*64 64x65 bf16 x24
```

The scores still start their last matmuls while POOL runs its 0.09. *Waits between first key and first value product*: the -1.8 did not shorten the stretch, 17.05 us against 16.80; the waits did shrink (PE busy 16.59 of 17.05, before 15.94 of 16.80), but more work stood in it. The second half of w_k landed at 33.1, not 34.1, ahead of the late start, so its +1.5 fell away. These two terms failed in opposite directions, so that the sum behind the start came out near is in part luck. (Slips in the sums, such as nine casts of 0.6 as 5.0, or 162.1 less 33.0 as 128.9, are 0.4 us or less and move nothing.)

**The rivals.** *The memset stuck in POOL's line*: POOL waited for PE (first row: sum, count, longest), and PE hardly for POOL (the page's groups, idle time at the end).

```profile
POOL scratch L1026 <- PE bank L923: 86.0, 23, 6.5
```

```profile
L923 PE MATMUL bank<-vb,e 64*64 64x65 bf16 x1088 | 20.7, 197 | 1.2 <-DVE kt L787 0.7 <-POOL scratch L1026 0.3
L923 PEld LDWEIGHTS <-e 64*64 64x64 bf16 x1088 | 16.3, 109 | 5.7 <-issue 2.3 <-POOL scratch L1026 1.6 <-DVE x L949 0.4
```

*The front wins* was the opposite of what happened. *The last keys*: toward the end the chain runs through a DMA transpose of q (130.50 to 135.19) and not of k, and behind the first key product PE has no gap of over 0.66 us. The rival that came true was missing: that the front is held by the attention ahead of the first key product, with the number of its instructions and POOL's constants among what it costs, which the part on the change didn't price at all.

**Would it have been visible?** The added constants on POOL, ahead of the identity, were in the order of the changed kernel, with prices in the trace of before (0.8 for three selects, 2.0 for hmask). The instruction count was in the order too. That a block of 256 costs PE a wait was not in the trace of before: its gaps at block ends are at most 0.2 us.

The first key product and the end move together, but loosely. Starts at 41.4 and 43.0 us went with 183.7 and 184.7, starts from 37.0 to 39.8 with 177.4 to 180.0, the front with the short queue (starts from 32.1 to 34.9) with 174.3 to 176.5, and the kernel before has 166.6 at 24.3. Against that, the two replanned kernels had 180.9 and 179.8 at 35.8 and 32.7, the one with the first key products early 179.2 at 33.7, and the one without two loads 179.6 at 35.9. So an earlier start is worth roughly 1 us for each, where it isn't lost behind it.
